# Summing late modulation vectors over partitions with a DMA transpose and a VectorE sum in place of one-column matmuls, and turning rows with full-width stationary tiles

## The chip, the cores and the metric

The kernel runs on one core of one Trainium2 chip. The metric is the device time of one execution in microseconds (us). I quote medians. "Span" is the time from the first to the last instruction in the trace; it is somewhat shorter than the device time. PE is the tensor engine and PEld its weight loads. PSUM is the memory that matmuls write their results into; in this program one of its banks is written anew only after another engine has read it out.

## The reference

An adaLN block: six modulation vectors of 1024 come from a conditioning row `c`, then linear attention and a SwiGLU feed-forward follow, each on a modulated layer norm.

```python
mod = (_silu(c) @ w_mod).reshape(1, 6, 1, -1)
sa, ca, ga, sb, cb, gb = mod[:, 0], ..., mod[:, 5]
h = _layernorm(x) * (1 + ca) + sa
x = x + ga * _A_ref(h, A_wqkv, A_wo)        # linear attention, 32 heads
h = _layernorm(x) * (1 + cb) + sb
x = x + gb * _B_ref(h, w_gate, w_up, w_down) # silu(h Wg) * (h Wu) @ Wd
# x: (1, 2048, 1024) bf16, F = 3584
```

The "late" vectors are `ga`, `cb`, `sb` and `gb`. Only these are touched here.

## The kernel before

The program is a list of instructions recorded in order. Each engine runs its own in that order and waits on semaphores for the others. All `P.*` calls go through one recording helper, so every instruction has the helper's line in the profile (L176), and one tells groups apart by their tiles.

A late vector is made on VectorE. `macc` multiplies a block of 128 rows of `w_mod` (one row per partition) by its `silu(c)` and adds it to `ACC`. After eight of these, `ACC[p, d]` still has to be summed over the 128 partitions. `macc_split` splits it into a high and a low bf16 part, and matmuls against a column of ones do the sum, with the data as the stationary tile:

```python
def macc_split():
    P.dve("tensor_copy", out=MHL[:, 0, :], in_=ACC[:])
    P.dve("tensor_tensor", out=MHL[:, 1, :], in0=ACC[:], in1=MHL[:, 0, :], op=ALU.subtract)

def mod_cols(bank, c0):
    for m in range(NDT):            # 8
        for i in range(2):
            P.pe("matmul", out=PS[:, bank, c0 + m:c0 + m + 1], lhsT=MHL[:, i, m * 128:(m + 1) * 128],
                 rhs=ONES[:, 0:1], start=(m == 0 and i == 0), stop=(i == 1), skip_group_check=True)

def mod_row_a(bank, c0, i):         # for ga and gb, which are needed as rows
    P.dve("tensor_copy", out=MROW[:, i, :], in_=PS[:, bank, c0:c0 + 8])

def mod_row_b(bank, i, dst):        # "row turn": 8 columns become 8 rows
    P.pe("matmul", out=PS[0:NDT, bank, 0:128], lhsT=MROW[:, i, :], rhs=IDENT[:], start=True, stop=True)
    P.dve("tensor_copy", out=MR8[0:NDT, i, :], in_=PS[0:NDT, bank, 0:128])
    # ... (written to DRAM and read back as a broadcast)
```

`z_row` turns the sum of the keys the same way, with two 8-column matmuls. The output projection loop (16 row tiles `st`) and the gate/up loop (28 groups `ft` a chunk) carry the side work:

```python
for st in range(NST):
    # ... two groups of 8 matmuls, each followed by a VectorE add that frees the PSUM bank
    if 1 <= st <= 4:
        macc(STGX[0], 2 * st - 2); macc(STGX[0], 2 * st - 1)
        if st == 4: macc_split()
    if st == 6:
        mod_cols(6, 0); mod_fin_col(6, 0, 3, False)
    if 8 <= st <= 15:
        macc(STGX[1], st - 8)
        # ... split at 15
# gate/up, first chunk: mod_cols and mod_row_a at ft == 3, mod_row_b at ft == 5
```

## Time and profile before

| | before |
|---|---|
| time, median of 3 | 834.51 us (834.47 to 834.51) |
| span of the profiled run | 832.1 us |
| mean granted clock | 1.000 |

The page's busy line, and its line for the chain of work that ended last:

```profile
PE 825.8 (99%) x4147; PEld 380.1 (46%) x4147; DVE 302.8 (36%) x662; ACT 196.3 (24%) x335; POOL 43.2 (5%) x56
...
PE 97%; DVE 2%; DMA 0%; issue 0%; POOL 0%; ACT 0%; DVEq 0%
```

The kernel is bound by PE. Work taken from PE counts; work given to another engine counts only where it makes PE wait. The view of the tile `mhl` shows the sums (columns: engine, operation, operands, count, shortest/median/longest ns, first and last start, shapes):

```profile
L176 PEld LDWEIGHTS ps<-ones,mhl x64: 95/96/99, 103.9 to 262.8; 128*128 128x128 bf16 x64
L176 PE MATMUL ps<-ones,mhl x64: 163/163/178, 104.1 to 262.8; 128*128 128x1 bf16 x64
L176 DVE CAST mhl<-acc x4: 674/693/695, 98.5 to 250.8; 128x1024 bf16<-128x1024 f32 x4
L176 DVE TENSOR_TENSOR mhl<-acc,mhl x4: 1224/1225/1226, 99.2 to 251.5; 128x1024 bf16<-128x1024 f32 x4
```

163 ns is the latency of one matmul, not what it costs in a stream. The timeline of PE around the first group (columns: start us, us, engine, operands, shape, count) shows the cost:

```profile
102.82 1.46 PE L176 MATMUL ps<-ht,wqk 128*128 128x512 bf16 x6
104.12 0.54 PE L176 MATMUL ps<-ones,mhl 128*128 128x1 bf16 x16
104.52 0.81 PE L176 MATMUL ps<-ht,wqk 128*128 128x512 bf16 x3
```

The group starts at 104.12 and the next 512-column matmul starts at 104.52, so sixteen matmuls push what follows back by 0.40 us. The same view around the first row turn:

```profile
121.35 0.59 PE L176 MATMUL ps<-ht,wqk 128*128 128x512 bf16 x2
121.88 0.22 PE L176 MATMUL ps<-ident,mrow 128*8 128x128 bf16 x1
122.03 0.60 PE L176 MATMUL ps<-ht,wqk 128*128 128x512 bf16 x2
```

The turn starts at 121.88 and what follows at 122.03. That is 0.15 us for a matmul with 128 columns to stream, and the turn itself began late as well: two 512-column matmuls that began at 121.35 have started 0.43 us later at their usual spacing of 0.216 us, at 121.78. At the third group I show the weight loads instead, because they carry the waits (in brackets: idle us before, and what ended it):

```profile
216.64 0.10 PEld L176 LDWEIGHTS ps<-ones,mhl 128*128 128x128 bf16 x1
216.91 0.44 PEld L176 LDWEIGHTS ps<-ones,mhl 128*128 128x128 bf16 x15 [0.17 <-DVE mhl L176]
217.52 0.55 PEld L176 LDWEIGHTS ps<-mw,pqt 128*128 128x128 bf16 x4 [0.17 <-DVE xres L176]
```

From the first load of this group to the first load after it, 0.88 us pass (216.64 to 217.52); at the first group it is 0.60 us (103.90 to 104.50 in the same view). So 0.28 us more, with two waits for VectorE: for the low part of `MHL`, and for a residual add that frees a bank. Last, how full VectorE is in two stretches (columns: stretch, then PE, PEld, DVE, ACT and POOL busy us with counts, clock, DMA share, GB/s):

```profile
115.00:127.00 12.00, 12.00 (x57) 5.29 (x55) 11.74 (x28) 7.60 (x14) 0.00 (x0) 1.00 0.37 47
...
190.00:250.00 60.00, 59.76 (x314) 27.82 (x313) 48.65 (x108) 20.01 (x35) 12.98 (x11) 1.00 0.66 191
```

A mean load of 36% hides that VectorE is full from 115 to 127 us.

### The profile page before, as it was taken

Reading aid. Unit: us, or ns where it says so; the run is one execution under the profiler, and the core shown is the slowest. Engines: PE = TensorE matmul, PEld = TensorE weight load, DVE = VectorE, ACT = ScalarE, POOL = GpSimd, SP = SyncE. Lnnn points to the kernel's source line nnn. Section 1 sums busy time; section 2 is a strip of 40 time slices with the busy share of each in tenths; the row PEclk is TensorE's granted clock in tenths of the full one; section 3 lists DMA queues with packets and bytes.
Section 4 is the critical chain, followed back from the end, with each engine's and each line's share of the span. In section 5 each row is a group of like instructions: output and inputs, shape, how many; then the busy total and the mean of one; then the engine's idle time right before and its main releaser. Section 6 shows DMA issues by size and latency. Waiting matters only on the chain.

```text
span 832.1 us, 10139 instructions
## 1 busy us (share of the span) xinstructions
PE 825.8 (99%) x4147; PEld 380.1 (46%) x4147; DVE 302.8 (36%) x662; ACT 196.3 (24%) x335; POOL 43.2 (5%) x56
## 2 busy tenths in 40 slices
PE   8999999999999999999999999999999999999998
PEld 4544444454444444444444444444444444444444
DVE  5797985657873222120221111122111212111111
ACT  3767642222332111110111111111111111111011
POOL 1000000000050000030000003000000300000000
PEclk9999999999999999999999999999999999999999
DMA  9969734928287885710455571045558004553000
GB/s 320 289 149 232 217 60 148 200 102 302 41 220 245 261 258 152 185 44 13 114 152 152 152 193 35 13 117 151 153 152 195 30 13 120 153 153 94 1 26 25
DMA packets 190924, 117.17 MB, mean 141 GB/s; under 512 B 49560, under 2 KB 174624, under 8 KB 190880
## 3 DMA queue, kind: packets, MB, share of 16 engines
q1 hardware_dynamic: 190864, 116.55, 51.5%
q8 instruction: 32, 0.52, 0.3%
q14 instruction: 12, 0.10, 0.0%
q10 hardware_dynamic: 16, 0.00, 0.0%
HBM read 100.67 MB, written 4.33 MB: 126 GB/s over the span
## 4 chain that ended last, share of the span: by engine, by line
PE 97%; DVE 2%; DMA 0%; issue 0%; POOL 0%; ACT 0%; DVEq 0%
PE ps L176 97%; DVE stats L176 0%; DVE xres L176 0%; DMA xres<-in_A_x_dram 0%; DVE acc L176 0%; DVE mhl L176 0%; DVE ve L176 0%; POOL rstd L176 0%; DVE mv L176 0%; ACT mw L176 0%; DVE ut L176 0%; DVE mean L176 0%; DVE msq L176 0%; DVE nmr L176 0%; DVE sumx L176 0%
## 5 line engine op out<-in xcount | busy, mean ns | idle before, releaser
L176 PE MATMUL ps<-h2t,gug 128*128 128x512 bf16 x896 | 211.7, 379 | 0.0
L176 PE MATMUL ps<-h2t,guu 128*128 128x512 bf16 x896 | 211.7, 379 | 0.0
L176 DVE TENSOR_TENSOR at<-sg,ps 128x512 bf16<-128x512 bf16 x112 | 77.0, 688 | 296.1 <-PE ps L176 296.1
L176 ACT ACTIVATE sg<-ps 128x512 bf16<-128x512 f32 x112 | 66.9, 597 | 310.3 <-PE ps L176 310.3
L176 PEld LDWEIGHTS ps<-h2t,guu 128*128 128x128 bf16 x896 | 87.7, 98 | 105.7
L176 PEld LDWEIGHTS ps<-h2t,gug 128*128 128x128 bf16 x896 | 87.5, 98 | 105.3
L176 PE MATMUL ps<-wd_a,at 128*128 128x512 bf16 (+2 forms) x528 | 113.5, 373 | 0.0
L176 PE MATMUL ps<-ht,wqk 128*128 128x512 bf16 x512 | 112.1, 379 | 0.1
L176 PE MATMUL ps<-wd_b,at 128*128 128x512 bf16 (+2 forms) x396 | 85.8, 373 | 0.0
L176 PEld LDWEIGHTS ps<-wd_a,at 128*128 128x128 bf16 x528 | 51.1, 98 | 59.8
L176 PEld LDWEIGHTS ps<-ht,wqk 128*128 128x128 bf16 x512 | 49.3, 98 | 58.4 <-issue 0.2
L176 DVE TENSOR_TENSOR ut<-att,gb_b 128x512 bf16<-128x512 bf16 (+1 forms) x32 | 14.4, 450 | 166.7 <-ACT att L176 166.7
L176 ACT ACTIVATE att<-ps 128x512 bf16<-128x512 f32 (+1 forms) x32 | 17.4, 591 | 182.1 <-PE ps L176 182.1
L176 PEld LDWEIGHTS ps<-wd_b,at 128*128 128x128 bf16 x396 | 38.3, 98 | 44.7
L176 PE MATMUL ps<-pk,xres 128*128 128x512 bf16 x256 | 56.7, 379 | 0.0
L176 PE MATMUL ps<-mw,pqt 128*128 128x512 bf16 x256 | 56.2, 379 | 0.1
L176 POOL TENSOR_SCALAR h2t<-h2t,modcol 128x512 bf16<-128x512 bf16 x32 | 28.4, 901 | 395.2 <-DMA h2t<-xn 378.8
L176 ACT ACTIVATE e<-ps 128x512 bf16<-128x512 f32 x56 | 33.2, 604 | 32.3 <-PE ps L176 24.1
L176 PEld LDWEIGHTS ps<-mw,pqt 128*128 128x128 bf16 x256 | 24.9, 98 | 29.7 <-DVE xres L176 0.2
L176 PEld LDWEIGHTS ps<-pk,xres 128*128 128x128 bf16 x256 | 24.8, 98 | 29.8 <-issue 0.4
L176 ACT ACTIVATE junk<-xres 128x1024 bf16<-128x1024 bf16 x24 | 25.4, 1058 | 36.0 <-DVE xres L176 35.8
L176 POOL TENSOR_TENSOR rstd<-ve,neghalf 128x1 f32<-128x1 f32 (+2 forms) x17 | 14.1, 842 | 214.9 <-DVE ve L176 174.8
(101 smaller groups left out, 343.7 us busy)
## 6 DMA issues: line engine op xcount, KB each, us to landing
gug<-in_B_w_gate_dram SPq DMA_DIRECT2D x56, 512.0 KB, 4.0
guu<-in_B_w_up_dram SPq DMA_DIRECT2D x56, 512.0 KB, 5.3
xres<-in_A_x_dram SPq DMA_DIRECT2D x20, 256.0 KB, 8.1
rb<-recip_den SPq DMA_DIRECT2D x8, 512.0 KB, 11.9
stgx<-in_w_mod_dram SPq DMA_DIRECT2D x2, 2048.0 KB, 7.9
wd_a<-in_B_w_down_dram SPq DMA_DIRECT2D x4, 1024.0 KB, 7.3
out_dram<-xres SPq DMA_DIRECT2D x31, 128.0 KB, 1.7
xres<-in_A_x_dram SPq DMA_DIRECT2D x3, 1024.0 KB, 12.9
```

The source lines that it names most:

```text
L176: return getattr(e, method)(**kw)
```

## The change

The intent is to take the four partition sums off PE. A DMA transpose turns `MHL` so that the partition becomes the free dimension, and VectorE sums rows. Row turns get a stationary tile of 128 columns, the unused ones zero. Accumulations and sums also move to other places in the loops.

```diff
-        ONES = T("ones", SM + 768, [128, 128], BF16)
+        ZHL = T("zhl", SM + 512, [128, 2, 128], BF16)
+        RED = T("red", SM + 2336, [128, NDT], FP32)
+        MHLT = T("mhlt", 192 * KB, [128, 2 * NDT, 128], BF16)
-        MROW = T("mrow", SM + 7776, [128, 2, NDT], BF16)
+        MROW = T("mrow", SM + 7936, [128, 128], BF16)
-        P.dve("memset", ap=ONES[:], constant=1.0)
# ... in macc_split
+            xbar(MHLT[:], MHL[:].rearrange("p i d -> p (i d)"))
-        def mod_cols(bank, c0):
# ... (16 one-column matmuls, gone)
+        def mod_red():
+            P.dve("tensor_reduce", out=RED[:], in_=MHLT[:].rearrange("d (i m) p -> d m i p", i=2),
+                  axis=mybir.AxisListType.XY, op=ALU.add)
# ... row turn
-            P.pe("matmul", out=PS[0:NDT, bank, 0:128], lhsT=MROW[:, i, :], rhs=IDENT[:], start=True, stop=True)
+            P.pe("matmul", out=PS[:, bank, 0:128], lhsT=MROW[:], rhs=IDENT[:], start=True, stop=True)
# ... the same in z_row, with ZHL; both tiles are zeroed once on GpSimd
+        add(s1, 7, lambda: P.pool("memset", ap=MROW[:], constant=0.0))
+        add(s1, 7, lambda: P.pool("memset", ap=ZHL[:], constant=0.0))
# ... output projection loop
-            if 1 <= st <= 4:
-                macc(STGX[0], 2 * st - 2)
-                macc(STGX[0], 2 * st - 1)
-                if st == 4:
-                    macc_split()
+            for kt in ((), (0,), (1,), (2, 3), (4,), (5,), (6, 7))[st] if st < 7 else ():
+                macc(STGX[0], kt)
             if st == 6:
-                mod_cols(6, 0)
-                mod_fin_col(6, 0, 3, False)
-            if 8 <= st <= 15:
-                macc(STGX[1], st - 8)
-                if st == 15:
-                    macc_split()
+                macc_split()
+            if st == 8:
+                mod_red()
+                mod_fin_col(3, False)
# ... gate/up loop, first chunk: macc(STGX[1], ft) at ft < 8, split at 8,
#     mod_red and mod_row_a at 11, mod_row_b at 12 (before: columns at 3, turn at 5)
```

More of the change, by code (lines that the diff above doesn't have):

```diff
@@ L328, in bass_adaLN_cond__linear_attn_block__swiglu_ffn__prompt_kernel @@
         ZCOL = T("zcol", SM + 2304, [128, NHG], FP32)
-        ZHL = T("zhl", SM + 2336, [128, 2, NHG], BF16)
+        RED = T("red", SM + 2336, [128, NDT], FP32)
         MASK4 = T("mask4", SM + 2368, [128, 4], BF16)
@@ L707, in macc_split, with mod_fin_col @@
             P.dve("tensor_tensor", out=MHL[:, 1, :], in0=ACC[:], in1=MHL[:, 0, :], op=ALU.subtract)
-        def mod_cols(bank, c0):
-            for m in range(NDT):
-                for i in range(2):
-                    P.pe("matmul", out=PS[:, bank, c0 + m:c0 + m + 1], lhsT=MHL[:, i, m * 128:(m + 1) * 128],
-                         rhs=ONES[:, 0:1], start=(m == 0 and i == 0), stop=(i == 1), skip_group_check=True)
-        def mod_fin_col(bank, c0, idx, plus_one):
-            P.dve("tensor_copy", out=MODTMP[:, 0:8], in_=PS[:, bank, c0:c0 + 8])
+            xbar(MHLT[:], MHL[:].rearrange("p i d -> p (i d)"))
+        def mod_red():
+            P.dve("tensor_reduce", out=RED[:], in_=MHLT[:].rearrange("d (i m) p -> d m i p", i=2),
+                  axis=mybir.AxisListType.XY, op=ALU.add)
+        def mod_fin_col(idx, plus_one):
+            P.dve("tensor_copy", out=MODTMP[:, 0:8], in_=RED[:])
             if plus_one:
@@ L720, in mod_fin_col, with mod_row_a @@
             P.dve("tensor_copy", out=MODCOL[:, idx, :], in_=MODTMP[:, 0:8])
-        def mod_row_a(bank, c0, i):
-            P.dve("tensor_copy", out=MROW[:, i, :], in_=PS[:, bank, c0:c0 + 8])
+        def mod_row_a():
+            P.dve("tensor_copy", out=MROW[:, 0:NDT], in_=RED[:])
         def mod_row_b(bank, i, dst):
-            P.pe("matmul", out=PS[0:NDT, bank, 0:128], lhsT=MROW[:, i, :], rhs=IDENT[:], start=True, stop=True)
+            P.pe("matmul", out=PS[:, bank, 0:128], lhsT=MROW[:], rhs=IDENT[:], start=True, stop=True)
             P.dve("tensor_copy", out=MR8[0:NDT, i, :], in_=PS[0:NDT, bank, 0:128])
@@ L836, in z_cols @@
             P.dve("tensor_reduce", out=ZCOL[:], in_=ZP[:], axis=mybir.AxisListType.X, op=ALU.add)
-            P.dve("tensor_copy", out=ZHL[:, 0, :], in_=ZCOL[:])
-            P.dve("tensor_tensor", out=ZHL[:, 1, :], in0=ZCOL[:], in1=ZHL[:, 0, :], op=ALU.subtract)
+            P.dve("tensor_copy", out=ZHL[:, 0, 0:NDT], in_=ZCOL[:])
+            P.dve("tensor_tensor", out=ZHL[:, 1, 0:NDT], in0=ZCOL[:], in1=ZHL[:, 0, 0:NDT], op=ALU.subtract)
             P.dve("tensor_tensor", out=ZSEL[:].rearrange("p (g x) -> p g x", x=36)[:, :, 0:4],
-                  in0=ZHL[:, 0, :].unsqueeze(2).to_broadcast([128, NHG, 4]),
+                  in0=ZHL[:, 0, 0:NDT].unsqueeze(2).to_broadcast([128, NHG, 4]),
                   in1=MASK4[:].unsqueeze(1).to_broadcast([128, NHG, 4]), op=ALU.mult)
@@ L879, in bass_adaLN_cond__linear_attn_block__swiglu_ffn__prompt_kernel @@
         add(s3, 14, macc_split)
-        add(s3, 2, lambda: mod_cols(7, 0))
-        add(s3, 3, lambda: mod_row_a(7, 0, 0))
+        add(s1, 7, lambda: P.pool("memset", ap=MROW[:], constant=0.0))
+        add(s1, 7, lambda: P.pool("memset", ap=ZHL[:], constant=0.0))
+        s3.setdefault(2, []).extend([mod_red, mod_row_a])
         add(s3, 12, lambda: mod_row_b(7, 0, GA_B))
@@ L911, in z_row @@
             for i in range(2):
-                P.pe("matmul", out=PS[0:NHG, 6, 0:128], lhsT=ZHL[:, i, :], rhs=IDENT[:], start=(i == 0), stop=(i == 1))
+                P.pe("matmul", out=PS[:, 6, 0:128], lhsT=ZHL[:, i, :], rhs=IDENT[:], start=(i == 0), stop=(i == 1))
             P.dve("tensor_copy", out=ZR8[0:NHG, :], in_=PS[0:NHG, 6, 0:128])
@@ L994, in bass_adaLN_cond__linear_attn_block__swiglu_ffn__prompt_kernel @@
             if g == 1:
+                mod_red()
+                mod_fin_col(2, True)
                 den()
-            if g == 3:
-                mod_cols(7, 0)
-                mod_fin_col(7, 0, 2, True)
             if 6 <= g <= 9:
@@ L1042, in th2_dma, with th2_mod @@
             xbar(H2T[:].rearrange("p dt (j s) -> p (dt j) s", j=4), XN2[:].rearrange("p dt j q -> p (dt j q)"))
+        def th2_mod():
             for dt in range(NDT):
@@ L1068, in bass_adaLN_cond__linear_attn_block__swiglu_ffn__prompt_kernel @@
                 ln2_sq(st - 1)
-            if 1 <= st <= 4:
-                macc(STGX[0], 2 * st - 2)
-                macc(STGX[0], 2 * st - 1)
-                if st == 4:
-                    macc_split()
-            if st == 6:
-                mod_cols(6, 0)
-                mod_fin_col(6, 0, 3, False)
-            if 8 <= st <= 15:
-                macc(STGX[1], st - 8)
-                if st == 15:
-                    macc_split()
+            for kt in ((), (0,), (1,), (2, 3), (4,), (5,), (6, 7))[st] if st < 7 else ():
+                macc(STGX[0], kt)
+            if st == 6:
+                macc_split()
+            if st == 8:
+                mod_red()
+                mod_fin_col(3, False)
             if st == 7:
@@ L1084, in bass_adaLN_cond__linear_attn_block__swiglu_ffn__prompt_kernel @@
                 th2_dma()
+            if st == 8:
+                th2_mod()
             if st == 7:
@@ L1110, in bass_adaLN_cond__linear_attn_block__swiglu_ffn__prompt_kernel @@
                     P.dma("wd%d" % i, wt, wdv[:, 4 * i:4 * i + 4, :])
-                if ch == 0 and ft == 3:
-                    mod_cols(6, 0)
-                    mod_row_a(6, 0, 1)
-                if ch == 0 and ft == 5:
+                if ch == 0 and ft < 8:
+                    macc(STGX[1], ft)
+                if ch == 0 and ft == 8:
+                    macc_split()
+                if ch == 0 and ft == 11:
+                    mod_red()
+                    mod_row_a()
+                if ch == 0 and ft == 12:
                     mod_row_b(6, 1, GB_B)
@@ L1119, in bass_adaLN_cond__linear_attn_block__swiglu_ffn__prompt_kernel @@
                 th2_dma()
+                th2_mod()
             for j in range(4):
```

## The prediction

> **What bounds it now.** The tensor engine. The profile's busy table gives PE 825.8 of 832.1 us (99%), the chain that ended last is 97% PE, and the granted clock is 1.000. VectorE is busy 36% of the span. So PE work removed counts in full, and VectorE or DMA work added counts only where it makes PE wait. VectorE is not idle everywhere: the table of stretches shows it busy 11.7 of 12 us at 115-127 us and 48.7 of 60 us at 190-250 us.
>
> **Removed from PE.** (1) Four groups of 16 one-column matmuls (timeline: about 104, 143, 217, 262 us). I take the distance from the end of the matmul before to the end of the last one: 0.38 us a group, 24 ns a matmul, the third 0.43. Sum about 1.55 us. The 163 ns that the groups view gives one of them is latency, not cost. The Trainium skill ("TensorE: Matmul & The Clock Gate", on the 56 ns gap) puts the least start-to-start at about 25 ns, and this trace agrees. (2) Three row turns have a stationary tile 8 columns wide (122, 131, 270 us; four matmuls). The first narrow matmul ends 93 ns late and the next full-width one 106 ns late, so 0.20 us a turn, 0.6 us in all. Full-width neighbours show only 216 ns per 512 columns, so I expect this to go. (3) After the third group PE waits about 0.25 us more for a VectorE add, because accumulations pile up there; they are now spread. PE gains 2.1 to 2.4 us in total.
>
> **Added, off PE.** Four DMA transposes of 128x2048 (the pk ones of that size land in 4.3 us, up to 6.3), and four VectorE sums over 2048 elements. The Trainium skill ("VectorE: DVE Perf Modes", perf-mode table) has tensor_reduce only at the 1x rate. The 1024-element 1x accumulation takes 1.28 us here, so my estimate is 2.3 us each. The last eight accumulations move to the first eight gate/up groups, where VectorE is nearly idle.
>
> **Critical path, place by place.**
> - About 105 us: the sum waits for its transpose (issued at about 100.5, landing about 105). The 2 MB load behind it on the queue moves from 97.3 to about 103, landing about 111 instead of 105; the first accumulation waits 1-3 us and VectorE runs 1-2 us late until 130. I estimate at least 0.4 us of bank slack left, so no PE wait.
> - About 131-138 us: hidden before the denominator finishes near 141.
> - About 222-230 us: the worst place. Two accumulations, the split, four normalisations and the sum come in a row; I estimate the sum ends at 230 and PE waits 0 to 0.5 us for the next add.
> - About 277-292 us: DMA is saturated (290-345 GB/s); the transpose has to land before about 289. The row turn then has only about 0.2 us of margin, and PE waits if the transpose is late.
>
> **Predicted:** 832.3 us (saving 2.2 us, 0.27%); 8 in 10 between 831.6 and 833.8. Faster by over 2%: 0.005; within 2%: 0.985; slower: 0.01.
>
> **What would show it.** No one-column matmuls on the modulation tiles. The matmul after a row turn shows no late end. Four reduces of about 2.3 us. PE idle up by under 0.5 us, if at all near 230 or 292 us. Busy PE time down about 2 us. Everything after 300 us as before, only earlier.
>
> **What would make it wrong.** A slow transpose under load (stall of up to 3 us at the last row turn); a reduce well over 2.3 us; the late 2 MB load starving the last accumulations, so that PE waits for a bank near 118 us; the narrow tile not being the cause of the 0.2 us around a row turn, which would leave 832.9.

## The result, and the profile after

| | before | after |
|---|---|---|
| time, median of 5 | 834.51 us (834.47 to 834.51) | 831.78 us (831.48 to 832.92) |
| span of the profiled run | 832.1 us | 829.7 us |
| time less span, all runs (before: those of the later jobs) | 2.2 us | 1.7 us |

The ratio is 0.997, 95% interval 0.9958 to 0.9982: a gain of 0.3%, clear of noise and inside 2%. The predicted 832.3 us was 0.5 us too high.

The page's busy line and its chain line, of the changed kernel:

```profile
PE 819.3 (99%) x4005; PEld 378.6 (46%) x4083; DVE 311.0 (37%) x665; ACT 196.3 (24%) x335; POOL 40.7 (5%) x58
...
PE 96%; DVE 2%; issue 1%; DMA 0%; ACT 0%; POOL 0%; DVEq 0%; ACTq 0%
```

Do not read the fall of PE from 825.8 to 819.3 us as 6.5 us gained. There are 4083 weight loads, 64 fewer than before as there should be, but only 4005 matmuls: in this trace about one record in fifty is missing. The weight loads are complete, so I compare the two traces by them. I line up the 4083 weight loads that both kernels have, in order, and look where the start of the later kernel's load, less that of the earlier one, changes for good. From 11 us on there are these steps and no others over 50 ns:

| place (us, before) | step | what stands there |
|---|---|---|
| 104, 143, 263 | -0.40 each | a group of 16 one-column matmuls gone |
| 217 | -0.68 | the same, and 0.28 more |
| 122, 131, 294 (turn at 270 before) | -0.20 each | row turn now full-width |
| 147 | +0.11 | PE waits (cause under e4) |
| 231 | +0.07 | PE waits for a late VectorE add |
| sum | -2.30 | |

(For the last turn the place moved: the comparison steps -0.20 where the old turn's delay and the new turn have both passed.) In the first 11 us the two traces differ back and forth, by 0.48 us at the first weight load and by up to 0.16 us after it, and the changed kernel comes out of this stretch 0.16 us ahead, which is not in the sum. Traces of the changed kernel and of its repeat (e0) differ there by up to half a microsecond; I take that as start-up and no part of the change.

The transposes and sums that replace the matmuls, in the view of the tile `mhlt`:

```profile
L176 SPq DMA_TRANSPOSE mhlt<-mhl x4: 1328/1814/3787, 100.3 to 280.6; - x4
L176 DVE TENSOR_REDUCE red<-mhlt x4: 2278/2282/2286, 104.7 to 289.0; 128x8 f32<-128x2048 bf16 x4
...
  DMA mhlt<-mhl: 3.3, 1
...
DMA to landing us min/median/max: 4.3/4.5/5.8
```

A sum takes 2.28 us. VectorE stood still for a transpose once, for 3.3 us, and PE has no wait for it. The row turn at 121 us in PE's timeline, to be read against the one before:

```profile
120.36 1.03 PE L176 MATMUL ps<-ht,wqk 128*128 128x512 bf16 x4
121.22 0.22 PE L176 MATMUL ps<-ident,mrow 128*128 128x128 bf16 x1
121.28 0.59 PE L176 MATMUL ps<-ht,wqk 128*128 128x512 bf16 x2
```

The turn now takes 0.06 us of the stream instead of 0.15, and starts on time. VectorE around the third sum, and at the last one:

```profile
226.13 2.28 DVE L176 TENSOR_REDUCE red<-mhlt 128x8 f32<-128x2048 bf16 x1
...
228.73 0.68 DVE L176 SCALAR_TENSOR_TENSOR xres<-ps,xres 128x512 bf16<-128x512 f32 x1
229.34 0.08 DVE L176 DVE_READ_ACCUMULATOR xres<-ps,xres 128x1 f32 x1
...
289.00 2.28 DVE L176 TENSOR_REDUCE red<-mhlt 128x8 f32<-128x2048 bf16 x1
291.32 0.17 DVE L176 CAST mrow<-red 128x8 bf16<-128x8 f32 x1
```

The add after the third sum ends at 229.4, and PE, which needs its bank, is late by 0.07 us there. The last sum's result is copied by 291.49, and the row turn starts at 291.65. The view of the tile `mrow` shows how little that leaves (a wait of the weight load, in us, and how often):

```profile
its engine sat idle before it (us, times) until:
  DVE mrow L176: 0.2, 1
```

And the two stretches again:

```profile
115.00:127.00 12.00, 11.95 (x57) 5.49 (x57) 11.72 (x28) 7.46 (x15) 0.00 (x0) 1.00 0.24 46
...
190.00:250.00 60.00, 59.52 (x286) 27.09 (x289) 43.11 (x106) 21.84 (x37) 10.73 (x12) 1.00 0.71 204
```

So the trace accounts for 2.30 us, while the time fell by 2.73. The remaining 0.43 us is not in the span: the time exceeds the span by about 2.2 us in runs of the kernel before (2.17 to 2.26 in the later jobs) and by about 1.75 in runs of the changed one (1.68 to 1.78), a difference of about 0.45. The first experiments look for the parts of the 2.30; the later ones for the other 0.45.

### The profile page after: what moved, and what is told of

It is laid out like the page before. It is cut to its first block, busy times and chain, and to the rows that moved or that the text cites. A ratio compares the mean times of both kernels' runs of the same rounds, so it can differ in the third digit from the quotient of the medians.

```text
span 829.7 us, 9938 instructions
## 1 busy us (share of the span) xinstructions
PE 819.3 (99%) x4005; PEld 378.6 (46%) x4083; DVE 311.0 (37%) x665; ACT 196.3 (24%) x335; POOL 40.7 (5%) x58
## 4 chain that ended last, share of the span: by engine, by line
PE 96%; DVE 2%; issue 1%; DMA 0%; ACT 0%; POOL 0%; DVEq 0%; ACTq 0%
PE ps L176 96%; DVE acc L176 1%; DVE stats L176 0%; DMA xres<-in_A_x_dram 0%; DVE pkt L176 0%; DVE e L176 0%; DVE xres L176 0%; DVE pqt L176 0%; POOL rstd L176 0%; DVE mv L176 0%; ACT mw L176 0%; ACT e L176 0%; DVE ve L176 0%; DVE ut L176 0%; DVE ht L176 0%
## 5 line engine op out<-in xcount | busy, mean ns | idle before, releaser
L176 POOL TENSOR_SCALAR h2t<-h2t,modcol 128x512 bf16<-128x512 bf16 x32 | 26.4, 843 | 383.2 <-DMA h2t<-xn 383.2
L176 DVE SCALAR_TENSOR_TENSOR xres<-ps,xres 128x512 bf16<-128x512 f32 x32 | 21.5, 688 | 12.2 <-PE ps L176 12.0
```

The lines of the kernel that those rows point to most:

```text
L176: return getattr(e, method)(**kw)
```

## The experiments

Twelve kernels, all correct. Runs e0 to e3 shared one chip (before there: 834.55 us, 9 runs), e4 to e7 another (834.59 us, 9 runs), and e8 to e11 a third (834.69 us, 7 runs). "Step" always means a step in the comparison of weight-load starts described above, taken from the profiled run.

### e0: the changed kernel again

> The changed kernel once more, as the yardstick for the other runs of this chip and for the spread of its times (5 runs lay between 831.48 and 832.92 us, while the kernel before lay within 0.04 us). My theory: the saving is 2.4 us of PE work that is no longer there plus a few tenths that wander, so about 831.8 us, saving 2.4 to 2.8. Rival: the saving of 2.7 us was partly luck of the runs; then it comes out near 832.5 or above. If the spread is a property of this kernel (DMA transposes or waits with no margin), it is over 0.5 us again; if it was an accident of the first job, it is gone.

Measured: 831.75 us (831.66 to 832.08), ratio 0.9967. The saving of 2.8 us stands. The medians of the spans of this job, 832.3 us before and 830.0 us here, give 2.3 us, so the 2.30 of the trace does not hang on one run. The spread is 0.4 us here and was 1.4 in the first job; before spreads over 0.65 us in this job and over 0.04 in the first. So the narrow range of the kernel before in the first job was the accident, not a property of it.

### e1: the row turns alone

```diff
 # on the kernel before
-    P.pe("matmul", out=PS[0:NDT, bank, 0:128], lhsT=MROW[:, i, :], rhs=IDENT[:], ...)
+    P.pe("matmul", out=PS[:, bank, 0:128], lhsT=MROW[:], rhs=IDENT[:], ...)   # and z_row; two GpSimd memsets; ONES only one column wide
```

> The kernel before, with only the row turns changed to full-width stationary tiles; the one-column matmuls stay. My theory: each of the three turns loses the 0.20 us that switching to a narrow tile and back costs, so 0.6 us less than before: 833.9 us, and in the trace the matmul after each turn ends 216 ns after the one before it instead of 323. Rival: the delay comes from the wait for the copy out of PSUM or from the turn itself, whatever its width; then the time stays at 834.5.

Measured: 833.45 us, 1.10 less than before (the ratio's interval, 0.9975 to 1.0000, just reaches no change). The steps are there: -0.20, -0.20 and -0.20 us, and none at the one-column groups. That is the 0.6 expected. The other 0.5 us was not: the time exceeds the span by 1.74 to 1.80 us in the runs of e1 and by 2.18 to 2.26 in those of before. This was the first sign that something outside the span differs.

### e2: the sums alone

```diff
 # on the changed kernel
-    P.pe("matmul", out=PS[:, bank, 0:128], lhsT=MROW[:], rhs=IDENT[:], ...)
+    P.pe("matmul", out=PS[0:8, bank, 0:128], lhsT=MROW[:, 0:8], rhs=IDENT[:], ...)   # and z_row
```

> The changed kernel with the row turns narrow again (8 columns). My theory: 0.6 us slower than the changed kernel, so about 832.4 us, and the steps of 0.20 us at the three turns are gone from the comparison of the weight-load times with before, while the four steps of 0.40 us stay. If the two parts of the change were not additive, the saving of this run and of the run with the rows alone would not sum to that of the whole change within about 0.3 us.

Measured: 832.35 us. Against the changed kernel the three turns step by +0.20, +0.20 and +0.21 us; against before the four groups step by -0.39, -0.40, -0.68 and -0.40. The two parts add up in the trace. They do not in the times (1.10 + 2.20 = 3.30 against 2.80), because both e1 and e2 have the 0.45 us outside the span.

### e3: the accumulations spread, one-column matmuls kept

```diff
 # on the kernel before: the changed kernel's places for the accumulations (and for th2_mod, GpSimd);
+    if st == 8: mod_cols(6, 0); mod_fin_col(6, 0, 3, False)   # was st == 6
+    if ch == 0 and ft == 10: mod_cols(6, 0); mod_row_a(6, 0, 1)   # was ft == 3; turn at 12
```

> The kernel before with only the new places of the accumulations for the third and fourth vector (spread over more row tiles, the last eight moved into the gate/up phase); one-column matmuls and narrow turns stay. My theory: the extra 0.28 us at the third group (its step is 0.68 where the others are 0.40) is a PE wait for a VectorE add that was late; with the accumulations spread it goes: 834.2 us, 0.2 to 0.35 less than before. Rival: the 0.28 us belongs to the one-column group itself (its weight loads and the switch); then the time stays at 834.5 and the 252 ns late end after the third group is still there.

Measured: 834.25 us, 0.30 less than before (the ratio's interval, 0.9982 to 1.0009, includes no change). The group now stands at 224 us, and the timeline of PE's weight loads there reads

```profile
223.23 0.53 PEld L176 LDWEIGHTS ps<-mw,pqt 128*128 128x128 bf16 x3
223.88 0.67 PEld L176 LDWEIGHTS ps<-ones,mhl 128*128 128x128 bf16 x16
224.48 0.77 PEld L176 LDWEIGHTS ps<-mw,pqt 128*128 128x128 bf16 x5
```

From the group's first load to the first load after it, 0.60 us pass, as at the first group, where the kernel before took 0.88 at this one; both brackets are gone. The steps say the same: -0.68 at the old place, +0.40 at the new one. The extra belonged to VectorE being late, not to the group.

### e4: an attempt to better the changed kernel

```diff
 # on the changed kernel
-P.dma("wo", WO[:], wov)                  # before the z row on the queue
+    if g == 0: z_row(); P.dma("wo", WO[:], wov)
-    for kt in ((), (0,), (1,), (2, 3), (4,), (5,), (6, 7))[st] ...   # split at 6, sum at 8
+    for kt in ((), (0,), (1, 2), (3, 4), (5,), (6, 7))[st] ...       # split at 5, sum and th2_mod at 9
```

> An attempt to better the changed kernel: the 2 MB weight load that stood before the broadcast of the z row on the DMA queue is issued after it, the third vector's split comes one row tile earlier and its sum one row tile later. My theory: the two PE waits that the changed kernel still shows (0.11 us at 146 us and 0.07 us at 230 us) go, so 0.1 to 0.2 us less than the changed kernel, about 831.6 us. Rival: those waits are only shifted to the next late add, and the time is that of the changed kernel, or the weight load comes late for the folding and costs more than 0.2 us.

Measured: 831.63 us (831.40 to 831.90), ratio to before 0.9964; the changed kernel had 831.75 and 0.9967 on another chip. The wait at 230 us is gone from its trace: against e4, the changed kernel, e0, e2, e6, e10 and e11 all step by +0.06 to +0.08 there. The wait at 146 us is gone too. It is also missing in e2, e6, e10 and e11, which keep the old order of the queue, but there it is missed narrowly, and the trace of the changed kernel shows where it comes from (SPq is the queue that issues the DMAs; `zb` is the z row's broadcast, `gtmp` is made from it, and `g` is the VectorE operation that empties a bank):

```profile
140.36 0.33 SPq L176 DMA_DIRECT2D zb<-z_row  x1
145.07 1.41 DVE L176 SCALAR_TENSOR_TENSOR g<-ps,modcol,gtmp 128x512 bf16<-128x512 f32 x2 [3.63 <-ACT gtmp L176]
145.88 2.70 PEld L176 LDWEIGHTS ps<-pk,xres 128*128 128x128 bf16 x14 [0.43 <-DVE g L176]
```

The kernel before issued the 2 MB load of `wo` at 127.41 us, the write of the z row at 131.38 and the broadcast at 135.66. Here `wo` stands behind the second transpose and goes out at 131.23, right before the write of the z row (132.52), and the broadcast goes out at 140.36, 7.8 us after the write. (e3, which has no transposes, issues `wo` at 127.74.) In e4, with `wo` behind them, the broadcast goes out at 134.25, 2.7 us after the write, and `g` starts at 141.36, 3.7 us earlier: there the wait is removed with room to spare. In the others PE merely arrives late enough or the broadcast lands early enough (in e2 PE is 0.43 us later at this place than in the changed kernel, and `g` starts at 144.97; in e10 it starts at 144.28). In time the gain of 0.07 us over e0, on another chip, is inside the spread: e4 is not shown to be faster.

### e5: each sum done twice

```diff
 # on the changed kernel, in mod_red
+    P.dve("tensor_reduce", out=RED[:], in_=MHLT[:]..., axis=mybir.AxisListType.XY, op=ALU.add)
```

> The changed kernel with each of the four VectorE sums done twice (same result). My theory of the slack: 2.28 us more of VectorE costs nothing at the first two places, and comes through nearly whole at the third (226 us, where a bank is freed late) and at the fourth (the row turn, 0.2 us of margin): 2.1 to 2.4 us each, so about 4.4 us more than the changed kernel, 836.2 us. Rival 1: VectorE is hidden everywhere because its mean load is 37%: under 0.5 us more. Rival 2: VectorE is full between 112 and 130 us, so the first place costs about 2 us as well: over 6 us more.

Measured: 837.03 us (836.02 to 838.03), 5.3 us over the changed kernel's median. Two of the five runs had a mean clock of 0.998 and are the two slowest. The trace has the clean answer. Against the changed kernel there is no step at 105 us, +0.17 at 146 us, +2.32 at 230 us and +2.23 at 291 us, 4.7 us in all; the profiled run lost 0.85 us more in the first 12 us. The +0.17 is not the second sum's: the first `g` waits 1.49 us for `gtmp` there, so it is the late broadcast described under e4. PE's timeline at the third and at the fourth sum:

```profile
227.62 2.97 PE L176 MATMUL ps<-mw,pqt 128*128 128x512 bf16 x13
232.81 3.41 PE L176 MATMUL ps<-mw,pqt 128*128 128x512 bf16 x15 [2.22 <-DVE xres L176]
```

```profile
293.26 1.89 PE L176 MATMUL ps<-h2t,guu 128*128 128x512 bf16 x8
297.20 0.23 PE L176 MATMUL ps<-ident,mrow 128*128 128x128 bf16 x1 [2.05 <-DVE mrow L176]
```

The bracket tells what PE stood idle for: a late VectorE add (its bank), and the copied sum (the row turn). So at these two places the changed kernel has next to no slack, while at the first two a further 2.28 us of VectorE is free. Both rivals fall, also the one that looked likely, that the stretch where VectorE is 98% busy would show the loss: there VectorE was at least 2.28 us ahead of what PE needed.

### e6 and e11: how wide a row turn's tile has to be

```diff
 # on the changed kernel; w = 32, 96, 120 in e6 and 40, 64, 72 in e11 (first, z row, last)
-    P.pe("matmul", out=PS[:, bank, 0:128], lhsT=MROW[:], rhs=IDENT[:], ...)
+    P.pe("matmul", out=PS[0:w, bank, 0:128], lhsT=MROW[:, 0:w], rhs=IDENT[:], ...)
```

> The changed kernel with stationary tiles of the row turns 32, 96 and 120 columns wide instead of 128 (first, z row, last). My theory: any width but the full one costs the same 0.20 us at a turn, because what costs is leaving the full-width form and coming back, not the number of columns; 0.6 us more than the changed kernel, like 8 columns. Rival 1: the cost goes with how narrow the tile is: about 0.15, 0.05 and 0.01 us. Rival 2: the cost depends on whether all four groups of 32 columns are used: 0.20 us for 32 and 96, none for 120.

> The changed kernel with stationary tiles of the row turns 40, 64 and 72 columns wide (first, z row, last). The widths 32, 96 and 120 cost 0.21, 0 and 0 us, so my theory that any narrower tile costs has fallen. New theory: [...]40 and 64 cost 0.20 us each and 72 nothing: 0.4 us more than the changed kernel. Rival 1: only a tile that fits in one strip of 32 columns costs: nothing at all three. Rival 2: the cost falls with the width: 0.15 and 0.1, and some at 72.

Steps against the changed kernel:

| columns | 8 (e2) | 32 | 40 | 64 | 72 | 96 | 120 | 128 |
|---|---|---|---|---|---|---|---|---|
| us | +0.20 | +0.21 | +0.21 | +0.22 | 0 | 0 | 0 | 0 |

PE's timeline at the z row (two matmuls), 96 columns in e6 and then 64 columns in e11:

```profile
130.20 0.81 PE L176 MATMUL ps<-pk,xres 128*128 128x512 bf16 x3
130.84 0.28 PE L176 MATMUL ps<-ident,zhl 128*96 128x128 bf16 x2
130.96 0.81 PE L176 MATMUL ps<-pk,xres 128*128 128x512 bf16 x3
```

```profile
131.08 0.81 PE L176 MATMUL ps<-pk,xres 128*128 128x512 bf16 x3
131.82 0.30 PE L176 MATMUL ps<-ident,zhl 128*64 128x128 bf16 x2
132.05 0.82 PE L176 MATMUL ps<-pk,xres 128*128 128x512 bf16 x3
```

The turn starts 0.64 us after the first of the three matmuls before it in the first view and 0.74 us after it in the second; the next work starts 0.12 us after the turn in the first and 0.23 in the second. So the 64-column turn loses about 0.1 us going in and 0.1 us coming out. Each width stood at one turn only, but 8 columns (e2) cost 0.20 us at all three, so it is not the place that decides. The weight loads show what is lost. At 8, 32, 40 and 64 columns the turn's first load starts together with its matmul (both at 122.92 us for 40 columns), and so does the load of the next 128-column tile. At 72, 96, 120 and 128 columns the turn's load starts 0.11 to 0.22 us before its matmul (293.48 against 293.59 us for 72), while the matmul before it still streams. So up to 64 columns the overlap of a weight load with the matmul before it is missing, on the way in and on the way out. My theory for e6, that any width but the full one costs, fell; so did "the narrower the dearer". The cost is a threshold between 64 and 72 columns and the same 0.2 us below it. The Trainium skill ("TensorEngine Tiling (Array Packing)", Tiling Modes, Key Properties) says that changing the tiling mode drains TensorE, and lists 128x32 and 128x64 among the modes. The threshold and the missing overlap fit that; that the tile's width chooses the mode, and that a drain is what costs, is my reading and not shown: the runs show the cost, the threshold and the missing overlap. In time, e6 had 831.84 us and e11 832.39 (831.91 to 833.41; its profiled run, the slowest, is 1.6 us behind the changed kernel by 45 us already, long before the first turn).

### e7: each one-column group twice

```diff
 # on the kernel before
-    for m in range(NDT):
+    for m in [*range(NDT)] * 2:
```

> The kernel before with every late group of 16 one-column matmuls done twice (64 more in all, same result). My theory: each costs its start-to-start distance of 24 ns, so 0.38 us a group more, 1.5 us in all: 836.0 us. Rival: a group has a fixed cost (switching from 512-column matmuls to one-column ones and back) and the matmuls within are nearly free; then well under 1 us more. The 163 ns of latency that the profile shows for one would give 10 us.

Measured: 835.99 us, 1.40 more than before. Steps: +0.40, +0.40, +0.17 and +0.40 us. At the third group the second sixteen hide in the wait for VectorE that was there anyway. 0.40 us for 16 is 25 ns each, with no fixed cost of a group to be seen. The Trainium skill ("TensorE: Matmul & The Clock Gate", on the 56 ns gap) gives about 25 ns as the least distance from start to start for small matmuls, and this trace agrees.

### e8, e9 and e10: the 0.45 us outside the span

```diff
 # e8, on the kernel before
-P.dve("memset", ap=ONES[:], constant=1.0)
+P.dve("memset", ap=ONES[:, 0:1], constant=1.0)
 # e9, on the kernel before, where the changed kernel has its two
+for _ in range(2): add(s1, 7, lambda: P.pool("memset", ap=DUMMY[:], constant=0.0))
 # e10, on the changed kernel, where the kernel before had its own
+P.dve("memset", ap=MROW[:], constant=1.0)
```

> The kernel before with one edit: the vector of ones, of which only one column is read, is set in that column alone instead of 128 columns (the change drops this memset, the second thing that VectorE does). It is about time outside the span of the trace: in the kernels with the wide memset (before, the spread alone, the doubled columns) the time is 2.2 us over the span, in all others 1.75, and the spans alone give a saving of 2.3 us for the change instead of 2.7. Theory A: the memset makes that difference: 0.45 us less than before, 834.1 us, and 1.75 us over the span. Theory B: the two memsets on GpSimd that the changed kernel adds make it: the time stays at 834.5, with 2.2 over the span.

> The kernel before with two memsets on GpSimd added at the place where the changed kernel has them, on a tile that nobody reads. Theory A (the wide memset on VectorE makes the 0.45 us outside the span): 834.5 us and 2.2 us over the span. Theory B (these memsets make it): 834.1 us and 1.75 us over the span.

> The changed kernel with a memset of 128x128 on VectorE put back where the kernel before had it, on a tile that is set again later. Theory A: 0.45 us more than the changed kernel, about 832.2 us, with 2.2 us over the span instead of 1.75. Theory B, or a third cause (a name, a layout, the number of instructions): 831.75 us and 1.75 over the span.

| | time us | time less span, us (all runs) |
|---|---|---|
| before, same job | 834.69 | 2.17 to 2.26 |
| e8, small memset | 834.61 | 2.17 to 2.25 |
| e9, two GpSimd memsets added | 834.05 | 1.71 to 1.78 |
| e10, wide memset put back | 831.88 | 1.75 to 1.81 |

Theory A, which I had thought likelier, fell in all three. Two memsets on GpSimd, on a tile that nobody reads, at 56 us, shorten the part of the device time outside the span by about 0.45 us and change nothing inside it (e9 ends 0.02 us off before in the comparison). The times alone would not show it (e9's ratio has the interval 0.9975 to 1.0009; one of e8's four runs, at a mean clock of 0.998, took 836.55 us): the difference of time and span does, without overlap. Why is not settled. The effect is before the first or after the last instruction of the trace, where no view reaches. The number of GpSimd instructions (56 on the busy line before, 58 after) is a candidate; no run tested another number. One more number goes with it: the pages count 12 packets on the DMA queue q14, kind "instruction", in before, e3, e7 and e8, and 13 to 15 in all the kernels with 1.75 us. That this is the cause is not shown.

## Why the prediction was right

The sum for PE was right term by term. Predicted and measured: four groups 1.55 against 1.60 us; three row turns 0.6 against 0.60; the late add at the third group 0.25 against 0.28; new waits 0 to 0.5 against 0.07 at 230 us, where I had put the worst place, none at the last row turn, and 0.11 at 146 us, where I had put none. In the span that makes a forecast of 2.2 and a measured 2.30 us (2.48 gained less 0.18 of waits). That the waits came out near what the forecast left for them, about 0.2 us, is partly luck: more than half arose at a place that it called hidden.

- **One-column matmuls.** Costing them by distance rather than by the 163 ns latency was the step that mattered: the latency would have forecast 10 us. e7 confirms 25 ns each.
- **Row turns.** The size was right and confirmed by e1 and e2. What makes them dear was left open in the prediction, which spoke only of a tile 8 columns wide; the runs show a threshold between 64 and 72 columns, so "full-width" is more than is needed.
- **The late add.** It was two late VectorE results, the low part of `MHL` as well as the add. e3 shows that spreading the accumulations does this alone, without any transpose.
- **VectorE.** The sum was estimated at 2.3 us from another 1x operation and took 2.28, which agrees with the Trainium skill ("VectorE: DVE Perf Modes", the perf-mode tier table: tensor_reduce at 1x only). The order of places was right: free at 105 and 133 us, without slack at 226 and 289 us (e5). The slack at 105 us was larger than the "at least 0.4 us" of the forecast: e5 used up 2.28 us more there and PE did not wait.
- **DMA.** The 2 MB load after the first transpose made VectorE wait until 110.7 us (forecast: landing about 111), and PE did not wait. The last transpose landed in time; transposes took 4.3 to 5.8 us.
- **What was missed.** The forecast subtracted PE time from the device time as if everything outside the span stood still. It did not: 0.45 us of the 2.73 come from two GpSimd memsets that I had counted as nothing (e9). Without them the time would have been about 832.2 us, next to the forecast. The wait at 146 us (0.11 us) was not foreseen either: the forecast followed VectorE's work between 131 and 138 us, but not what the second transpose moves on the DMA queue, the `wo` load and behind it the z row's broadcast (e4).

## What to carry to other kernels

In a kernel bound by PE, cost small matmuls by how far they push the next full one back, from the starts in the timeline, and not by their recorded duration; then a change that takes 64 of them off PE is seen beforehand to be worth 1.6 us and not 10. When work moves to an engine with a low mean load, look for the one or two places where that engine's result is needed within the next few microseconds: doubling the work there shows at once which places have slack. Where the new work includes a DMA, look also at what stands behind it on its queue. And pad narrow stationary tiles in a stream of full-width ones to more than 64 columns; here that was 0.2 us each time.

## What the Trainium skill lacked or had wrong

- "TensorEngine Tiling (Array Packing)" says that a change of tiling mode drains TensorE but gives no cost, and does not say that a plain matmul with few columns pays it. Here a turn with 8, 32, 40 or 64 stationary columns among 128-column ones cost 0.20 to 0.22 us in all (there and back), one with 72, 96 or 120 nothing.
- "TensorE: Matmul & The Clock Gate" (LDWEIGHTS) gives the load time as columns over 1.2 GHz. The recorded load of a row turn's tile took 82 to 85 ns at 8 columns, 93 at 32, 95 at 40, 106 to 109 at 64, 109 at 72, 123 at 96 and 129 at 120 columns: about 0.4 ns a column on top of some 80 ns (my estimate from these), where the page's formula would give 0.83 ns a column from nothing (an estimate). At 128 columns it is only 95 to 99 ns.
- I found no page that says that device time outside the traced span can move with the program: two added GpSimd memsets took it from 2.2 to 1.75 us, with nothing changed inside the span.
